# Idle matmuls in the opening of a two-stage kernel, and the token keys of its second group moved ahead of the third's

## The chip, the core and the metric

The kernel runs on one core of a Trainium2 chip. A core has a matrix engine (TensorE, PE in the rows, with its weight loads as PEld), a vector engine (DVE), a scalar engine (ACT), a third elementwise engine (POOL), and an engine that here only issues transfers (SP). Each works through its own list of instructions in order and waits on semaphores for the others. The metric is the device time of one execution in microseconds; the kernel before takes 529.84 us, the median of three runs (529.17 to 530.13).

## The reference

The first stage is a linear attention over 4 batches, 8 heads, 768 steps and head size 48; its output is the input of a gated network with 3072 tokens, model width 384 and inner width 1536.

```python
for t in range(S):
    cur = einsum('bhd,bhe->bhde', u[None] * k[:, :, t], v[:, :, t])
    y[:, :, t] = einsum('bhd,bhde->bhe', r[:, :, t], state + cur)
    state = w[None, :, :, None] * state + einsum('bhd,bhe->bhde', k[:, :, t], v[:, :, t])
x = y.transpose(0, 2, 1, 3).reshape(B * S, H * D)
gate = 1 / (1 + exp(-(x @ w_gate)))
out = (gate * (x @ w_val)) @ w_out
```

All of it is in float32.

## The kernel before

The 768 steps are cut into 12 chunks of 64. One chunk of one half of the heads is a group, so there are 24 groups; they are numbered 0, 1, 2, ... in the order in which they are worked on. For each group n the following steps exist, and the letters are those of the table `START` in the code:

- `L` and `X` load its channels (queries and keys with the channel on the partitions, tile `chan`) and its tokens (keys and values with the token on the partitions, tile `toks`).
- `A`, `R`, `k`, `T` scale them by powers of the decay: bonus keys on ACT (line 287), queries on POOL or DVE (line 293), keys on DVE (line 304), token keys on POOL or DVE (line 308). `T` writes its result over the keys in `toks`.
- `Z` computes the scores on PE (line 375), `K` copies those under the mask to the tile `score` on DVE (line 383).
- `I` applies them to the values, from group 2 on with the part that comes from the state, and `O` forms the outer product of token keys and values for the next state; both are on PE at line 337. `O` needs the token keys of `T`.
- `h` and `l` round the output to the high part of the network's input on ACT (line 474) and take the rest as the low part on DVE (line 478); `s` and `d` renew and decay the state; `F` moves some rows of the input to other partitions by six transfers (line 482).

The network works in 12 blocks f of the inner width. `W` loads the block's weights, which come as whole 64-bit words, `c` (ACT, line 240) and `j` (DVE, line 247) turn them to float32, `w` (ACT, line 255) rounds them to a high part and `o` (POOL or DVE, line 258) forms the low part. `U` is the up projection, 18 matmuls at line 516: nine for the gate and nine for the value, each a product of a high or low part of the weights with a high or low part of the input. `g`, `m`, `H`, `q` are the gating on ACT, DVE, ACT and POOL or DVE, and `D` is the down projection (line 554). For the first two blocks the first tile of 512 tokens is worked on in two halves of 256, since its second half is computed later.

The order of the work is written out by hand. The first part of it, up to the end of the first 512 tokens, is the table `START`, a list of steps that are issued one after the other; each engine gets its instructions in this order and keeps it. Then a loop goes through the other five tiles of tokens with a fixed pattern: up projection, the attention of a later group in the first, fourth, seventh and tenth block, gating, and the down projection of the block before. In the listing `tc` is the step that makes the constants, the identity matrix `ident` among them, `tt` four transposes for the table of token powers on PE (line 197), and `tn` the copy of that table, which every `T` needs.

Of the loads, SP issues all. The scheduling layer gives the transfers eight semaphores in turn, and a transfer is issued when the one eight places ahead of it has landed.

Of the kernel before, what the change touches and what calls it, by code (L numbers as in the profile page):

```python
# [10 lines left out]
F32 = mybir.dt.float32  # L11
# [32 lines left out]
L.0 W.0 L.1 X.0 W.1 L.2 X.1 X.2 tc A.0 tk ti.1 R.0 ti.0 k.0 tp tr Z.0 tt K.0 I.0 c0.0 A.1 c0.1 tn  # L44
h.0 c.1 T.2 T.1 k.1 Rv.1 j0.1 l.0 Tv.0 j0.0 Z.1 O.0 W.2 F.0 W.3 L.3 L.4 W.4 X.3 j.1 K.1 I.1 O.1 A.2
w0.0 sa.0 w.1 h.1 w0.1 o0.1 o.1 R.3 Rv.2 k.2 o0v.0 l.1 s.1 Z.2 K.2 U.0 I.2 O.2 g.0 c.2 d.2 A.3 m.0
U.1 H.0 g.1 h.2 j.2 k.3 s.2 l.2 q.0 T.3 m.1 F.2 L.5 W.8 X.4 L.6 W.5 W.6 L.7 X.5 F.1 X.6 L.8 W.7 Z.3
K.3 I.3 O.3 w.2 A.4 k.4 H.1 c.3 h.3 l.3 R.4 D.0 Z.4 U.2 d.3 s.3 g.2 c.4 j.3 w.3 j.4 qv.1 m.2 o.2
U.4 H.2 g.4 w.4 A.5 K.4 q.2 U.3 D.2 g.3 Rv.5 m.3 k.5 ov.3 m.4 T.4 I.4 O.4 Z.5 H.3 A.6 d.4 h.4 H.4
c.6 c.5 k.6 s.4 K.5 l.4 Tv.5 j.6 R.6 q.3 D.1 D.3 U.5 I.5 g.5 h.5 j.5 qv.4 l.5 m.5 o.4 Z.6 D.4 R.7  # L50
O.5 U.6 A.7 d.5 H.5 K.6 k.7 s.5 q.5 T.6 w.5 ov.5 U.7 c.8 c.7 g.6 j.7 m.6 L.9 X.8 ub Y.8 W.9 W.10
X.7 I.6 Z.7 O.6 D.5 w.6 g.7 ov.6 d.6 w.7 H.6 s.6 j.8 qv.6 h.6 l.6 m.7 w.8 ov.7 H.7 qv.7 D.6 U.8 K.7
R.8 c.9 ov.8 g.8 m.8 Tv.7 H.8 U.9 qv.8 g.9 k.8 j.9 w.9 o.9 m.9 D.7 U.10 g.10 H.9 c.10 j.10 m.10 q.9
D.8 I.7 H.10 d.7 Z.8 O.7 h.7 w.10 D.9 s.7 U.11 ov.10 l.7 W.11 F.5 X.9 F.6 F.3 F.7 F.4 Y.9 qv.10
g.11 c.11 j.11 D.10 U.12 m.11 w.11 R.9 ov.11 U.13 g.12 H.11 qv.11 m.12 H.12 qv.12 g.13 t.8 D.11 b.8
i.8 D.12 K.8 k.9 m.13 H.13 q.13 b.9 T.9 t.9 i.9 T.8
# [4 lines left out]
def rwkv_then_moe(ctx: ExitStack, tc: tile.TileContext, wd, ub, ch, tk, rt, wt, rk0, vn0, wd0, out):  # L61
# [38 lines left out]
    def load_channels(n):  # L100
        c, g = GROUPS[n]
        chan[n] = ach.tile([P, 2, 512], F32, name="chan")
        nc.sync.dma_start(out=chan[n], in_=ch[c, g])  # L103

    def load_tokens(n):
        c, g = GROUPS[n]
        toks[n] = atk.tile([P, 2, TKW], F32, name="toks")
        nc.sync.dma_start(out=toks[n], in_=tk[c, g])  # L108
# [15 lines left out]
    def constants():  # L124
        make_identity(nc, ident)
        nc.gpsimd.memset(causal, 0.0)
# [7 lines left out]
        for t in score:  # L134
            nc.gpsimd.memset(t, 0.0)
        nc.gpsimd.memset(state, 0.0)
        nc.scalar.activation(table, ident[:, 0:1], AF.Sigmoid)
        nc.vector.memset(tops[0].rearrange("q n two -> q (n two)").bitcast(F32), 0.0)
        nc.gpsimd.memset(tops[1].rearrange("q n two -> q (n two)").bitcast(F32), 0.0)


# [109 lines left out]
    def round_weights(f, c):  # L251
# [3 lines left out]
        nc.scalar.copy(out=whi[f][:, c], in_=w32[f][:, c])  # L255
# [34 lines left out]

    def queries(n, eng=nc.gpsimd):
# [210 lines left out]
    class Moe:  # L502
# [3 lines left out]

        def up(self, f):
            w = whi[f], wlo[f]
            self.pair[f] = []
            for g in range(2):  # L510
                o = one_bank()
                self.pair[f].append(o)
                k = 0
                for kt in range(3):
                    for a, b in PASS:
                        nc.tensor.matmul(  # L516
                            o[:, self.cols], w[a][:, g * DM + kt * P : g * DM + (kt + 1) * P],
                            self.x[:, kt, b, self.cols], start=(k == 0), stop=(k == 8),
                        )
                        k += 1  # L520
# [73 lines left out]
    halves = [(0, g) for g in range(HALF)] + [(1, g) for g in range(HALF)] + [(2, g) for g in range(HALF, NF)]  # L594
    items = [(0, h, f) for h, f in halves]
    n0 = len(items)
# [24 lines left out]
    def idle_matmuls(k):  # L621
        t = pacc.tile([P, 512], F32, name="acc2")
        for _ in range(k):
            nc.tensor.matmul(t[:, 0:P], ident, ident, start=True, stop=True)

    steps = {
        "b": own_tokens, "i": diagonal, "ub": lambda: load_bonus(),
        "N": idle_matmuls,
        "L": load_channels, "X": load_tokens, "Y": load_own, "W": load_weights, "A": bonus_keys, "R": queries, "t": turn_queries,
        "k": keys, "T": token_keys, "Z": scores, "K": keep, "I": apply, "O": outer,  # L630
        "d": decay_state, "s": add_state, "h": x_high, "l": x_low, "F": fills, "D": finish,
# [260 lines left out]
```

## Time and profile before

| what | value |
|---|---|
| time, median of 3 runs | 529.84 us (529.17 to 530.13) |
| the profiled execution's own time | 529.63 us |
| its span, from the first to the last instruction | 527.8 us |
| PE busy | 506.9 us, 96% of the span |
| PEld, DVE, ACT, POOL busy | 422.0, 202.7, 186.2, 188.4 us |
| DMA queue of the loads, share of 16 engines | 25.3% |

The span is 1.8 us shorter than the time of the same execution; the rest lies ahead of the first and behind the last instruction. Times in rows count from the start of the span. In a timeline a row merges instructions of one kind that follow each other: start, time from the first's start to the last's end, engine, line, operation, operands, shape and count, and in brackets the idle time ahead of them with what ended it. A float32 matmul of a score or an outer product stands in the program once and in the trace as two records, so a group of 16 matmuls shows as x32.

### The profile page before, as it was taken

What the parts mean: (1) busy time and instruction counts of PE and PEld (TensorE: products, weight loads), DVE (VectorE), ACT (ScalarE), POOL (GpSimd) and SP (SyncE); (2) the same over time, 40 slices, a digit from 0 to 9 for tenths busy, and PEclk for the clock granted to TensorE, in tenths of its full rate; (3) what the DMA queues carried; (4) which work ended last, traced back from release to release, by engine and by line L of the source; (5) the groups of instructions that cost most, each with busy time, mean ns of one, the idle gap of its engine ahead of it and who ended that gap; (6) DMA issues with size and microseconds to landing.
All of it is one profiled execution on the core that took longest, in us unless ns stands there. A gap on an engine that the chain in (4) does not pass through costs nothing.

```text
span 527.8 us, 11947 instructions
## 1 busy us (share of the span) xinstructions
PE 506.9 (96%) x5204; PEld 422.0 (80%) x5204; DVE 202.7 (38%) x345; ACT 186.2 (35%) x395; POOL 188.4 (36%) x158
## 2 busy tenths in 40 slices
PE   3689999999999999999999999999999999999995
PEld 3679888888888788888888888888888888888884
DVE  8877856555242243242341432331442211111112
ACT  5587764544223134233233332331432221211211
POOL 4463512314555252453442452552353111111220
PEclk9999999999999999999999999999999999999998
DMA  8939744122212030420230420311400000100001
GB/s 328 363 131 418 268 170 187 24 85 84 79 74 76 22 107 2 145 87 17 81 102 8 146 88 0 98 37 71 147 17 2 11 10 11 61 0 1 0 2 65
DMA packets 15579, 47.84 MB, mean 91 GB/s; under 512 B 2368, under 2 KB 4928, under 8 KB 14112
## 3 DMA queue, kind: packets, MB, share of 16 engines
q1 hardware_dynamic: 15376, 46.74, 25.3%
q8 instruction: 43, 0.70, 0.6%
q10 hardware_dynamic: 144, 0.26, 0.1%
q14 instruction: 16, 0.13, 0.1%
HBM read 39.92 MB, written 4.72 MB: 85 GB/s over the span
## 4 chain that ended last, share of the span: by engine, by line
PE 94%; DMA 2%; SPq 1%; DVE 1%; issue 1%; POOL 0%; ACT 0%; DVEq 0%; POOLq 0%
PE ring L516 56%; PE acc L554 29%; PE ring L337 7%; PE sc L375 2%; DMA toks<-in_tk 2%; DVE xt L478 0%; DVE score L383 0%; POOL toks L308 0%; SPq L233 0%; SPq L103 0%; SPq L108 0%; ACT xt L474 0%; DVE sg L567 0%; SPq L95 0%; ACT sg L525 0%
## 5 line engine op out<-in xcount | busy, mean ns | idle before, releaser
L516 PE MATMUL ring<-xt,wx 128*128 128x512 f32 (+1 forms) x1332 | 308.1, 385 | 0.7 <-ACT sg L525 0.5
L516 PEld LDWEIGHTS ring<-xt,wx 128*128 128x128 f32 x1332 | 246.7, 189 | 50.5 <-ACT sg L525 0.7
L538 POOL TENSOR_TENSOR h<-sg,h 128x512 fp32r<-128x512 f32 (+1 forms) x65 | 87.2, 1342 | 253.8 <-ACT h L534 253.8
L554 PE MATMUL acc<-h,wx 128*128 128x512 f32 (+1 forms) x666 | 161.3, 387 | 0.0
L554 PEld LDWEIGHTS acc<-h,wx 128*128 128x128 f32 x666 | 121.2, 188 | 24.9 <-DVE h L538 0.2
L529 DVE TENSOR_TENSOR sg<-ring,sg 128x512 f32<-128x512 f32 (+1 forms) x74 | 50.0, 675 | 237.5 <-PE ring L516 236.0
L525 ACT ACTIVATE sg<-ring 128x512 f32<-128x512 f32 (+1 forms) x74 | 43.3, 585 | 155.3 <-PE ring L516 155.3
L534 ACT CAST h<-sg 128x512 fp32r<-128x512 f32 (+1 forms) x74 | 45.0, 608 | 144.2 <-DVE sg L529 138.0
L293 POOL TENSOR_TENSOR dec<-chan,tabk 128x512 f32<-128x512 f32 x21 | 27.8, 1325 | 13.8 <-PE ring L337 13.7
L478 DVE TENSOR_TENSOR xt<-ring,xt 112x256 fp32r<-112x256 f32 (+1 forms) x52 | 19.9, 418 | 32.8 <-ACT xt L474 32.7
L308 POOL TENSOR_TENSOR toks<-toks,tabn 128x384 f32<-128x384 f32 x19 | 24.8, 1308 | 11.5 <-DMA toks<-in_tk 11.5
L314 POOL TENSOR_TENSOR dec<-dec,toks 128x384 f32<-128x384 f32 x16 | 16.3, 1018 | 26.4 <-DMA dec<-in_rt 26.3
L375 PE MATMUL sc<-dec,chan 48*64 48x64 f32 x768 | 17.4, 231 | 7.7 <-DVE chan L304 7.6
L304 DVE TENSOR_TENSOR chan<-chan,tabk 128x512 f32<-128x512 f32 x24 | 24.7, 1027 | 0.1
L383 DVE COPY_PREDICATED score<-masks,sc 128x512 f32<-128x512 int32 x32 | 23.9, 746 | 1.8 <-PE sc L375 1.1
L428 ACT ACTIVATE state<-state,pw 112x96 f32<-112x96 f32 x80 | 23.4, 363 | 1.9 <-PE ring L337 1.8
L337 PE MATMUL ring<-score,toks 64*48 64x64 f32 (+1 forms) x768 | 16.7, 226 | 5.0 <-DVE score L383 4.1
L375 PEld LDWEIGHTS sc<-dec,chan 48*64 48x64 f32 x768 | 15.0, 145 | 8.1 <-POOL dec L293 7.6
L247 DVE SCALAR_TENSOR_TENSOR wf<-wr,top 128x1152 int32<-128x1152 int32 (+1 forms) x13 | 17.3, 1342 | 10.4 <-ACT top L240 6.9
L447 DVE TENSOR_TENSOR state<-state,ring 48x192 f32<-48x192 f32 (+1 forms) x52 | 17.9, 350 | 8.4 <-PE ring L337 4.6
L474 ACT CAST xt<-ring 112x256 fp32r<-112x256 f32 (+1 forms) x52 | 16.7, 364 | 9.0 <-PE ring L337 8.8
L337 PEld LDWEIGHTS ring<-score,toks 64*48 64x48 f32 (+1 forms) x768 | 14.3, 134 | 6.4 <-DVE score L383 4.8
(59 smaller groups left out, 247.1 us busy)
## 6 DMA issues: line engine op xcount, KB each, us to landing
wr<-in_wt SPq DMA_DIRECT2D x11, 1152.0 KB, 8.8
chan<-in_ch SPq DMA_DIRECT2D x24, 512.0 KB, 4.3
toks<-in_tk SPq DMA_DIRECT2D x24, 400.0 KB, 5.0
out_y<-wf SPq DMA_DIRECT2D x16, 256.0 KB, 2.4
dec<-in_rt SPq DMA_DIRECT2D x16, 192.0 KB, 2.7
xt<-xt SPq DMA_DIRECT2D x30, 64.0 KB, 2.3
wr<-in_wt SPq DMA_DIRECT2D x2, 576.0 KB, 5.2
xt<-xt SPq DMA_DIRECT2D x12, 32.0 KB, 3.9
```

The source lines that it names most:

```text
L293: eng.tensor_tensor(v4(t[:, 0]), v4(chan[n][:, 0]), bc2(table_of(n)[:, :, ::-1]), ALU.mult)
L304: nc.vector.tensor_tensor(v4(k), v4(k), bc2(table_of(n)), ALU.mult)
L308: eng.tensor_tensor(v4(k), v4(k), bc2(tabn[:, 4 * g : 4 * g + 4]), ALU.mult)
L337: nc.tensor.matmul(yb[n][bank][64 * half : 64 * half + m, cs], lhsT, rhs, start=first, stop=stop, skip_group_check=True,)
L375: nc.tensor.matmul(sc[64 * gm : 64 * gm + 64, be, o : o + C], kk[row, cs : cs + C], rr[row, cs : cs + C], start=True, stop=True,)
L383: nc.vector.copy_predicated(t.rearrange("q (b m i) -> q b m i", b=2, m=4), masks[:, m].bitcast(I32).unsqueeze(1).unsqueeze(1).broadcast_to ...
L516: nc.tensor.matmul(o[:, self.cols], w[a][:, g * DM + kt * P : g * DM + (kt + 1) * P], self.x[:, kt, b, self.cols], start=(k == 0), stop=(k ...
L525: nc.scalar.activation(sg[:, c], self.pair[f][0][:, c], AF.Sigmoid, scale=UP)
L529: nc.vector.tensor_tensor(sg[:, c], self.pair.pop(f)[1][:, c], sg[:, c], ALU.mult)
L534: nc.scalar.copy(out=h[:, 0, c], in_=sg[:, c])
L538: eng.tensor_tensor(h[:, 1, c], self.sg.pop(f)[:, c], h[:, 0, c], ALU.subtract)
L554: nc.tensor.matmul(self.acc[d][:, self.cols], w[a][:, 2 * DM + d * P : 2 * DM + (d + 1) * P], h[:, b, self.cols], start=(f == 0 and k == 0 ...
```

## The change

Four things in the code are different.

- The table `START` gets 30 matmuls of the identity with itself (step `N`, function `idle_matmuls`, which was there and was not used): 13 ahead of the first scores, then 3, 2, 1, 6, 2, 1 and 2 in front of the transposes, the scores of group 1, the outer product of group 0, the applied scores of group 1, its outer product, the scores of group 2 and the first up projection. They write to the bank of the third accumulator, which nothing reads before the first down projection starts it anew.
- In the table the token keys of group 1 (`T.1`) come before those of group 2 (`T.2`); before it was the other way round.
- The step that makes the constants is split into small ones, named one by one in the table in the same order on each engine; the up projection is split into its gate part `u` and value part `v`; and blocks are named by block and half (`0a`, `0b`, `2`) and not by a running number. Some functions take the engine as an argument, with the old one as default.
- Far later, ACT issues one copy of the state ahead of one rounding of the gated product; they changed places.

The diff, with the table cut to its first lines:

```diff
 START = """
-L.0 W.0 L.1 X.0 W.1 L.2 X.1 X.2 tc A.0 tk ti.1 R.0 ti.0 k.0 tp tr Z.0 tt K.0 I.0 c0.0 A.1 c0.1 tn
-h.0 c.1 T.2 T.1 k.1 Rv.1 j0.1 l.0 Tv.0 j0.0 Z.1 O.0 W.2 F.0 W.3 L.3 L.4 W.4 X.3 j.1 K.1 I.1 O.1 A.2
+ta L.0 tov.0 tc tb W.0 ts.0 L.1 ts.1 X.0 tz W.1 tk L.2 X.1 to.1 ti.1 X.2 ti.0 A.0 R.0 N.13 W.2 k.0
+c0.0 tp Z.0 tr N.3 tt A.1 K.0 I.0 c0.1 k.1 tn Rv.1 h.0 N.2 j0.1 Z.1 l.0 N.1 Tv.0 O.0 j0.0 c.1 N.6
+A.2 j.1 w0.0 T.1 sa.0 F.0 T.2 W.3 K.1 w.1 Rv.2 I.1 N.2 k.2 O.1 N.1 o0v.0 L.3 L.4 Z.2 W.4 N.2 X.3 h.1
...
-        def up(self, f):
-            w = whi[f], wlo[f]
-            self.pair[f] = []
-            for g in range(2):
-                o = one_bank()
...
+        def up_one(self, f, g):
+            w, o, k = (whi[f], wlo[f]), one_bank(), 0
+            self.pair.setdefault(f, []).append(o)
...
+        def up(self, f):
+            self.up_one(f, 0)
+            self.up_one(f, 1)
...
     def idle_matmuls(k):
-        t = pacc.tile([P, 512], F32, name="acc2")
+        t = accs[0][2] if 0 in accs else pacc.tile([P, 512], F32, name="acc2")
         for _ in range(k):
             nc.tensor.matmul(t[:, 0:P], ident, ident, start=True, stop=True)
...
+    moe_steps = {
+        "U": Moe.up, "u": lambda m, f: m.up_one(f, 0), "v": lambda m, f: m.up_one(f, 1), "g": Moe.sigmoid, "m": Moe.product, "H": Moe.h_high, "q": Moe.h_low,
+        "qv": lambda m, f: m.h_low(f, nc.vector),
     }
     for step in START.split():
         name, _, arg = step.partition(".")
-        steps[name](*([int(arg)] if arg else []))
+        if name == "D":
+            finish(block(arg))
+        elif name in moe_steps:
+            moe_steps[name](moe_of(block(arg)), block(arg)[2])
+        else:
+            steps[name](*([int(arg)] if arg else []))
```

On PE at the start of the program, before (line 375 is the first scores, 197 the transposes, 337 the applied scores of group 0):

```order
L887 UNCONDITIONAL_BRANCH
L375 MATMUL sc<-dec,chan 64x64 x16
L375 MATMUL sc<-chan,dec 64x64 x16
L197 MATMUL acc_201<-spare,sg 128x128 x4
L337 MATMUL ring<-score_97,toks 64x64 x2
```

and now (line 636 is the idle matmuls; 389, 204 and 351 are the old 375, 197 and 337):

```order
L917 UNCONDITIONAL_BRANCH
L636 MATMUL acc_161<-spare 128x128 x13
L389 MATMUL sc<-dec,chan 64x64 x16
L389 MATMUL sc<-chan,dec 64x64 x16
L636 MATMUL acc_218<-spare 128x128 x3
L204 MATMUL acc_222<-spare,sg 128x128 x4
L351 MATMUL ring<-score_97,toks 64x64 x2
```

Nothing that stood there changed places; the idle matmuls stand between.

On PE from the applied scores of group 1 (`score_98`) to the first up projection, before:

```order
L337 MATMUL ring<-score_98,toks 64x64 x2
L337 MATMUL ring<-score_98,toks 48x64 x2
...
L337 MATMUL ring<-toks 64x48 x2
L337 MATMUL ring<-toks 48x48 x2
...
L375 MATMUL sc<-dec,chan 64x64 x16
L375 MATMUL sc<-chan,dec 64x64 x16
L516 MATMUL ring<-xt,wx 128x256 x18
```

and now (526 is the old 516, the up projection):

```order
L636 MATMUL acc_320<-spare 128x128 x6
L351 MATMUL ring<-score_98,toks 64x64 x2
L351 MATMUL ring<-score_98,toks 48x64 x2
...
L636 MATMUL acc_371<-spare 128x128 x2
L351 MATMUL ring<-toks 64x48 x2
L351 MATMUL ring<-toks 48x48 x2
...
L636 MATMUL acc_391<-spare 128x128
L389 MATMUL sc<-dec,chan 64x64 x16
L389 MATMUL sc<-chan,dec 64x64 x16
L636 MATMUL acc_433<-spare 128x128 x2
L526 MATMUL ring<-xt,wx 128x256 x18
```

Again the old matmuls keep their order, with eleven idle ones between them.

On POOL, with the tiles' numbers, before (`toks_123` are the tokens of group 1, `toks_125` those of group 2, line 258 the low part of the first blocks' weights):

```order
L293 TENSOR_TENSOR dec_145<-chan_110,tabk_102 128x512
L308 TENSOR_TENSOR toks_125<-toks_125,tabn_103 128x384
L308 TENSOR_TENSOR toks_123<-toks_123,tabn_103 128x384
L258 TENSOR_TENSOR wx_358<-wf_242,wx_358 128x576
L258 TENSOR_TENSOR wx_362<-wf_315,wx_362 128x1152
```

and now (`toks_148` are the tokens of group 1, `toks_152` those of group 2):

```order
L307 TENSOR_TENSOR dec_155<-chan_114,tabk_102 128x512
L322 TENSOR_TENSOR toks_148<-toks_148,tabn_103 128x384
L322 TENSOR_TENSOR toks_152<-toks_152,tabn_103 128x384
L265 TENSOR_TENSOR wx_334<-wf_262,wx_334 128x576
L265 TENSOR_TENSOR wx_350<-wf_332,wx_350 128x1152
```

The two token keys changed places; all else on POOL, and everything on DVE and SP, stands as before.

## Rows read from the trace of the kernel before

**Rows 1.** Page, part 1: busy us, share of the span, instructions

```profile
PE 506.9 (96%) x5204; PEld 422.0 (80%) x5204; DVE 202.7 (38%) x345; ACT 186.2 (35%) x395; POOL 188.4 (36%) x158
```

**Rows 2.** The chain that ended last: start us, us, what

```profile
20.41 1.15 PE ring L337 x24
...
33.76 0.76 DVE score L383
...
38.83 8.72 PE ring L516 x54
```

**Rows 3.** Stretches: length, busy of each engine (records), granted clock, DMA share, GB/s

```profile
60.00:80.00 20.00, 19.82 (x284) 16.18 (x275) 14.05 (x21) 15.06 (x29) 5.14 (x4) 1.00 0.51 186
...
7.62:15.33 7.71, 6.98 (x196) 6.14 (x196) 7.14 (x15) 5.19 (x13) 0.00 (x0) 1.00 1.03 422
24.13:26.86 2.73, 2.73 (x12) 2.73 (x13) 2.11 (x4) 0.82 (x2) 2.73 (x2) 1.00 1.03 396
...
30.35:33.76 3.41, 2.94 (x95) 2.60 (x98) 2.31 (x7) 3.19 (x9) 3.06 (x3) 1.00 0.04 10
```

**Rows 4.** Timeline of PE from the first scores to the first down projection

```profile
7.62 1.13 PE L375 MATMUL sc<-dec,chan 48*64 48x64 f32 x32 [7.62 <-DVE chan L304]
...
17.59 1.12 PE L337 MATMUL ring<-score,toks 64*64 64x64 f32 x32 [2.25 <-DVE score L383]
...
24.14 3.36 PE L516 MATMUL ring<-xt,wx 128*128 128x256 f32 x16 [0.18 <-DVE xt L478]
27.43 0.68 PE L337 MATMUL ring<-dec,state 48*64 48x64 f32 x32
...
35.35 0.68 PE L337 MATMUL ring<-score,toks 64*64 64x64 f32 x32 [1.19 <-DVE score L383]
```

**Rows 5.** Lines 516 and 197: duration ns min/median/max, first and last start

```profile
L516 PE MATMUL ring<-xt,wx x10: 415/415/416, 24.5 to 26.4; 128*128 128x256 f32 x10
...
L516 PE MATMUL ring<-xt,wx x9: 279/282/389, 29.5 to 30.5; 128*128 128x256 f32 x9
...
L197 PE MATMUL acc<-spare,sg x4: 417/418/473, 9.5 to 10.2; 128*128 128x128 f32 x4
```

**Rows 6.** Timeline of DVE, ACT and POOL around the same work

```profile
1.02 0.29 POOL masks.py:199 TENSOR_SCALAR_AFFINE_SELECT spare<-spare 128x128 f32<-128x128 f32 x1
...
14.11 2.02 DVE L247 SCALAR_TENSOR_TENSOR wf<-wr,top 128x576 int32<-128x576 int32 x2
16.05 1.49 DVE L383 COPY_PREDICATED score<-masks,sc 128x512 f32<-128x512 int32 x2
...
17.49 2.86 POOL L308 TENSOR_TENSOR toks<-toks,tabn 128x384 f32<-128x384 f32 x2 [10.52 <-DMA toks<-in_tk]
18.01 1.49 DVE L304 TENSOR_TENSOR chan<-chan,tabk 128x512 f32<-128x512 f32 x1
...
21.57 1.51 ACT L474 CAST xt<-ring 48x256 fp32r<-48x256 f32 x4 [3.88 <-PE ring L337]
22.35 1.73 DVE L478 TENSOR_TENSOR xt<-ring,xt 48x256 fp32r<-48x256 f32 x4 [1.39 <-ACT xt L474]
23.86 4.04 POOL L258 TENSOR_TENSOR wx<-wf,wx 128x576 fp32r<-128x576 f32 x2 [3.51 <-ACT wx L255]
24.76 1.54 DVE L383 COPY_PREDICATED score<-masks,sc 128x512 f32<-128x512 int32 x2
...
27.86 1.27 POOL L293 TENSOR_TENSOR dec<-chan,tabk 128x512 f32<-128x512 f32 x1
27.94 2.41 DVE L247 SCALAR_TENSOR_TENSOR wf<-wr,top 128x1152 int32<-128x1152 int32 x1
```

**Rows 7.** Transfers issued at 4.69, 17.53 and 22.52: KB, us to landing

```profile
toks<-in_tk SPq DMA_DIRECT2D x1, 400.0 KB, 10.4
...
xt<-xt SPq DMA_DIRECT2D x1, 32.0 KB, 4.6
...
toks<-in_tk SPq DMA_DIRECT2D x1, 400.0 KB, 8.9
```

More of the change, by code (lines that the diff above doesn't have):

```diff
@@ L122, in rwkv_then_moe, with identity, causal_masks @@
     table = const.tile([P, 1], F32, name="table")
-    def constants():
+    def identity():
         make_identity(nc, ident)
+    def causal_masks():
         nc.gpsimd.memset(causal, 0.0)
@@ L133, in constants, with clear_scores, clear_state, first_table @@
             nc.gpsimd.tensor_copy(masks[lo : lo + 64, 1], ident[lo : lo + 64, lo : lo + 64])
-        for t in score:
-            nc.gpsimd.memset(t, 0.0)
-        nc.gpsimd.memset(state, 0.0)
+    def clear_scores(i, eng=nc.gpsimd):
+        eng.memset(score[i], 0.0)
+    def clear_state(eng=nc.gpsimd):
+        eng.memset(state, 0.0)
+    def first_table():
         nc.scalar.activation(table, ident[:, 0:1], AF.Sigmoid)
-        nc.vector.memset(tops[0].rearrange("q n two -> q (n two)").bitcast(F32), 0.0)
-        nc.gpsimd.memset(tops[1].rearrange("q n two -> q (n two)").bitcast(F32), 0.0)
+    def clear_top(i, eng=nc.gpsimd):
+        eng.memset(tops[i].rearrange("q n two -> q (n two)").bitcast(F32), 0.0)
     pw = const.tile([P, N2, 97], F32, name="pw")
@@ L249, in join_words, with round_weights @@
         )
-    def round_weights(f, c):
+    def round_weights(f, c, copy=nc.scalar.copy):
         if f not in wparts:
@@ L254, in round_weights @@
             whi[f], wlo[f] = wparts[f][:, 0:W3], wparts[f][:, W3 : 2 * W3]
[L255 removed]
+        copy(out=whi[f][:, c], in_=w32[f][:, c])
     def rest_of_weights(f, c, eng=nc.gpsimd):
@@ L470, in x_of, with x_high @@
         ]
-    def x_high(n):
+    def x_high(n, copy=nc.scalar.copy):
         for x, y in x_of(n, 0):
-            nc.scalar.copy(out=x, in_=y)
+            copy(out=x, in_=y)
     def x_low(n):
@@ L505, in __init__ @@
             self.pair, self.sg, self.h = {}, {}, {}
-        def up(self, f):
-            w = whi[f], wlo[f]
-            self.pair[f] = []
-            for g in range(2):
-                o = one_bank()
[L512 to L520, printed above, removed]
+        def up_one(self, f, g):
+            w, o, k = (whi[f], wlo[f]), one_bank(), 0
+            self.pair.setdefault(f, []).append(o)
+            for kt in range(3):
+                for a, b in PASS:
+                    nc.tensor.matmul(
+                        o[:, self.cols], w[a][:, g * DM + kt * P : g * DM + (kt + 1) * P],
+                        self.x[:, kt, b, self.cols], start=(k == 0), stop=(k == 8),
+                    )
+                    k += 1
+        def up(self, f):
+            self.up_one(f, 0)
+            self.up_one(f, 1)
         def sigmoid(self, f):
@@ L591, in store_last @@
             )
-    halves = [(0, g) for g in range(HALF)] + [(1, g) for g in range(HALF)] + [(2, g) for g in range(HALF, NF)]
-    items = [(0, h, f) for h, f in halves]
-    n0 = len(items)
+    items = [(0, 2, NF - 1)]
     for ti in range(1, len(TILES)):
@@ L641, in rwkv_then_moe, with block @@
         "Rv": lambda n: queries(n, nc.vector), "Tv": lambda n: token_keys(n, nc.vector),
[L642 to L647 removed]
+    }
+    def block(arg):
+        return (0, "ab".index(arg[-1]), int(arg[:-1])) if arg[-1] in "ab" else (0, 2, int(arg))
+    moe_steps = {
+        "U": Moe.up, "u": lambda m, f: m.up_one(f, 0), "v": lambda m, f: m.up_one(f, 1), "g": Moe.sigmoid, "m": Moe.product, "H": Moe.h_high, "q": Moe.h_low,
+        "qv": lambda m, f: m.h_low(f, nc.vector),
     }
@@ L672, in rwkv_then_moe @@
     load(n + 2)
-    for i in range(n0, len(items)):
+    for i in range(1, len(items)):
         ti, h, f = items[i]
```

91 lines of the change are left out of this document (51 added, 40 removed).

## The prediction

> **What bounds the kernel now.** I read the page first: PE is busy for 506.9 of 527.8 us [rows 1], so only its remaining 21 us, and matmuls that run slower than they could, can be won. Then the stretches: from 60 us on PE is busy for 19.8 of 20 us and more [rows 3], and in the chain of waits PE work follows PE work from 38.83 us on [rows 2]. So what the opening gives is read at that place: if the block at 38.83 us starts earlier by some time and nothing behind it runs dry, the kernel ends earlier by as much. Ahead of it the chain runs through the token keys on POOL, a pair that starts at 17.49 us when the tokens of group 2 have landed [rows 6] and in which those of group 1 stand second, and the outer product of group 1 at 20.41 us [rows 2].
>
> Third, the timeline of PE with the durations. A group of 32 records of the small matmuls takes 1.13 us at 7.62 and 0.68 us at 27.43 [rows 4]. Up to 26.4 us the matmuls of 256 columns start every (26.4 - 24.5)/9 = 0.21 us, and from 29.5 us every (30.5 - 29.5)/8 = 0.12 us [rows 5]. [...] The column of the granted clock reads 1.00 all the while [rows 3], so here only the durations tell the level. From 24.13 to 26.86 us PE was busy without a break with matmuls of 128 x 128 weights and 256 columns [rows 3, 4], and after that the rate is the high one.
>
> **The change part by part.** *Renamed steps, split constants, u and v.* Every engine but PE, POOL and ACT keeps its list, and ACT's one swap lies where PE never idles: nothing.
>
> *Thirteen idle matmuls at the start.* The identity is made at 1.02 + 0.29 = 1.3 us [rows 6], and the first scores wait for DVE until 7.62 us [rows 4], so PE has 6.3 us free. The trace of before has no idle matmul; the nearest is the four transposes of 128 columns, spaced by (10.2 - 9.5)/3 = 0.23 us at the low level [rows 5]. A float32 matmul leaves two records where a transpose leaves one. So one idle matmul costs between 0.23 and 0.46 us at the low level and half of that at the high one, and 13 cost at most 6.0 us: done at 7.3 us, in free time. I take the upper value.
>
> *Seventeen in the pauses.* At the high level 0.23 us each. Twelve (3, 2, 1, 6) stand ahead of the applied scores of group 1, 2.8 us against a pause of 2.25 us there [rows 4], 7.71 - 6.98 = 0.73 us of pauses ahead of it [rows 3], and six groups that each shrink by 1.13 - 0.68 = 0.45 us: covered. Two (0.46 us) stand between applied scores and outer product of group 1, where nothing hides them once the pause there is gone. One stands ahead of the scores of group 2, two ahead of the up projection, where other waits end later (below).
>
> *Token keys swapped, with the high level kept.* DVE ends the scores' copy for group 1 at 16.05 + 1.49 = 17.54 us, as before: its list ahead is full, behind weights that have to land. The applied scores take 17.59 to 18.27, the two idle ones end at 18.73. The tokens of group 1 land at 4.69 + 10.4 = 15.1 us [rows 7]. Its token keys then meet the joining of weights on DVE, 14.11 to 16.13 us, and end by 17.5 us even if they start only behind that (half of the pair's 2.86 us is 1.4 us [rows 6], so from 16.1 to 17.5). So the outer product runs from 18.73 to 19.4 us, where before it started at 20.41. ACT's cast, which waits for it, starts at 19.4 in place of 21.57 us, 2.2 us earlier, and DVE's low part, now 22.35 to 24.08 us, ends at 21.9.
>
> The first up projection needs this, the scores of group 2 ahead of it on PE, and the six moved rows. The keys of group 2 end at 18.01 + 1.49 = 19.5 us as before; the scores take two groups, 19.6 to 20.8, two idle ones to 21.3. The last moved rows land at 17.53 + 4.6 = 22.1 us [rows 7], which the change can't move, as they queue behind weights; only the seventh matmul needs them, and starting with the third at 21.9 it comes at 22.3. Sixteen matmuls of 0.12 us end at 24.0 us, where the sixteen of before end at 27.5 [rows 4]: 1.5 us of this is the level, the rest the earlier start. The copy of the next scores on DVE ended at 24.76 + 1.54 = 26.30 us, 2.2 us behind the low part [rows 6], so now at 24.1. The applied scores of group 2 start at 24.1 and not at 27.43: **3.3 us earlier**.
>
> From there the path forks. POOL's two weight parts (23.86 + 4.04 = 27.90 us) start behind ACT, 2.2 us earlier, so they end at 25.7, and the queries behind them at 27.0 us. The next joining of weights on DVE took 2.41 us beside those queries; the second one of the row at 14.11 has the same 1152 columns, twice those of the first, and took two thirds of 2.02, or 1.35 us, with POOL idle [rows 6]. So the queries blocked it, and again it ends 1.2 us behind them, at 28.2 us, 2.2 us earlier than 27.94 + 2.41 = 30.35. From there to the copy of the scores of group 3, at 33.76 us [rows 2], DVE was busy for 2.31 of 3.41 us and else waited for PE and ACT [rows 3], which now are 3.3 us ahead. So that copy can start at 28.2 + 2.3 = 30.5 us. That is **3.2 us earlier**, and the applied scores of group 3 start at 32.1 in place of 35.35 us [rows 4]. Their outer product, half a microsecond behind, needs tokens that land at 22.52 + 8.9 = 31.4 us whatever PE does [rows 7]; with 1.4 us at most on POOL they are ready by 32.8, just in time. That caps any gain near 3.4 us. The second set of moved rows, and the loads queued behind it on SP, wait for a low part on DVE that stands between the joining and that copy, so they come 2.2 to 3.2 us earlier.
>
> So the block at 38.83 us starts between 2.2 (if the loads decide) and 3.2 us (if PE does) earlier. I take the middle, **2.7 us**: 529.63 - 2.7 = 526.9 us against the profiled execution's own time, and as the median of the runs is 0.2 us above that, **527.1 us**.
>
> *Who goes first on DVE and POOL.* The joining at 27.94 us, begun 0.08 us behind POOL's queries, took 2.41 and not 1.35 us, and so did the keys at 18.01 us, 1.49 us beside the pair of token keys [rows 6]: of two such instructions the earlier one goes first. At 15.1 us DVE's joining (from 14.8) is ahead of the token keys, if nothing delays it. If POOL is first, the joining ends 1.0 us later, 1.2 of the 2.2 us at the cast are left, and the end comes near **528.0 us**. [...]
>
> **The rivals.** *The level is never lifted early, and the idle matmuls stand in the way (slower).* For it: from 7.62 to 15.33 us PE was busy for 6.98 of 7.71 us and the next group still took 1.12 us [rows 3, 4]: the level had not risen. Against it: what ran ahead of the rise were matmuls with 128 x 128 weights, and so are the idle ones. Price: at 0.46 us each the twelve ahead of the applied scores of group 1 take 5.5 us against 2.25 + 0.73 us of pauses, so these start 2.5 us late, at 20.1; with two more (0.9) the outer product starts at 22.1, 1.7 us late in spite of the swap, and three more (1.4) bring the up projection to some 2.5 us behind 24.14. At 0.23 us the twelve fit the pauses and nothing is lost. I take 1.4 us, a little over the middle: **531.0 us**. It decides from the point where the applied scores of group 1 start after 18.6 us, since from there their outer product, 1.8 us behind, is no earlier than it was.
>
> *Lifted at the start, lost again before the first up projection.* For it: pauses of up to 1.8 us remain, ahead of the applied scores of group 1. Against it: after the pause of 1.19 us at 35.35 the matmuls still ran at the high rate [rows 4]. [...] Price: applied scores 17.6 to 18.7, two idle ones at 0.46, outer product to 20.7 where it ended at 21.5, so 0.8 us are won at the cast; then two groups of scores (2.0) and three idle ones (1.4) fill PE until 24.1, and the 16 matmuls take 3.36 us as before. Between 0.5 us won and 0.5 us lost is left: **529.8 us**, the median of before.
>
> **How the numbers follow.** The forecast has a chance of 0.70, POOL winning the port 0.06, the level lost again 0.13, the idle matmuls in the way 0.11. What the measurement can tell from no change is about 0.2%, 1.06 us, so faster means below 528.8. Faster: 0.68 of the first, 0.05 of the second, 0.01 of the third, 0.74. The same: 0.02 + 0.01 + 0.11 + 0.02 = 0.16. Slower: 0.10. The forecast's own range is 526.1 (the cap of 3.4 us, and the 0.4 us by which runs differ) to 528.2; to hold 8 in 10 it reaches to the rival that loses the level: 526.1 to 529.9 us.
>
> **What would show it.** Right: the first scores take 0.7 us per group, the outer product of group 1 starts near 18.7, the first up projection spaces its matmuls by 0.12 us and ends near 24.0, and the steady stretch, now from 38.83 us, begins near 36 us. Wrong: small groups of 1.1 us behind the first idle matmuls, the cast still near 21.6 us, or new pauses of PE behind 38 us, where loads that didn't move would be late.

## The result, and the profile after

The changed kernel takes 537.34 us (median of 6 runs, 535.97 to 539.45), the kernel before beside it 529.59 us: the ratio is 1.0146, with a 95% interval of 1.0129 to 1.0162. It is slower by 1.5%, where 527.1 us was forecast and 526.1 to 529.9 given as the range. The profiled execution took 535.97 us, with a span of 534.2 us, the fastest of the six; against the 527.8 us of before 6.4 us are to be found in it.

The page's first part answers to [rows 1]: thirty float32 matmuls are 60 records more, and PE is busy for 8 us more. The fetches of instructions have a queue of their own in the third part of the page.

```profile
PE 514.9 (96%) x5264; PEld 427.7 (80%) x5264; DVE 203.2 (38%) x345; ACT 186.2 (35%) x395; POOL 188.9 (35%) x158
...
q8 instruction: 43, 0.70, 0.5%
```

The timeline of PE after, for the places of [rows 4]: start, length, line, what, and in brackets the idle time ahead of it and what ended it.

```profile
1.37 5.92 PE L636 MATMUL acc<-spare 128*128 128x128 f32 x26 [1.37 <-POOL spare masks.py:199]
7.63 0.69 PE L389 MATMUL sc<-dec,chan 48*64 48x64 f32 x32 [0.34 <-issue]
...
19.05 0.68 PE L351 MATMUL ring<-score,toks 64*64 64x64 f32 x32 [2.73 <-DVE score L397]
...
23.61 2.18 PE L526 MATMUL ring<-xt,wx 128*128 128x256 f32 x16 [0.25 <-DVE xt L492]
25.72 0.68 PE L351 MATMUL ring<-dec,state 48*64 48x64 f32 x32
...
33.06 0.43 PE L351 MATMUL ring<-dec,state 48*48 48x64 f32 x12 [0.74 <-issue]
...
50.62 0.98 PE L568 MATMUL acc<-h,wx 128*128 128x256 f32 x6
54.58 2.40 PE L568 MATMUL acc<-h,wx 128*128 128x256 f32 x12 [2.97 <-issue]
...
81.03 0.73 PE L568 MATMUL acc<-h,wx 128*128 128x512 f32 x2 [0.46 <-ACT h L548]
...
107.49 1.38 PE L526 MATMUL ring<-xt,wx 128*128 128x512 f32 x5 [1.11 <-DVE xt L492]
```

The rate of PE, the level of the prediction, is lifted as forecast: the first scores take 0.69 us per group, not 1.13. The first up projection ends at 25.8 us, 1.7 us earlier than before, though not at 24.0. The chain of waits then shows what became of it; it answers to the last row of [rows 2], and its first row to the last transfer of [rows 7].

```profile
24.15 9.18 DMA toks<-in_tk
...
38.05 8.72 PE ring L526 x54
...
51.61 2.97 issue
```

The tokens of group 3, issued at 24.15 us and not at 22.52, land at 33.3 us, 2.0 us later than before, and of the 1.7 us won at the up projection the block that started at 38.83 us keeps 0.78: it starts at 38.05. At 51.61 us PE stops in the middle of a down projection, between its sixth and seventh record of 18, for 2.97 us, labelled "issue": it waited for no semaphore that the profile shows. The stretches around it (length, then busy time of PE, PEld, DVE, ACT and POOL with their records, granted clock, DMA share, GB/s):

```profile
44.00:51.60 7.60, 7.45 (x196) 6.95 (x195) 5.78 (x10) 6.15 (x18) 4.71 (x5) 1.00 1.01 424
51.61:54.58 2.97, 0.00 (x1) 0.00 (x0) 2.30 (x6) 0.00 (x0) 2.46 (x1) 1.00 1.06 413
54.58:58.42 3.84, 3.84 (x16) 3.52 (x16) 1.68 (x2) 3.29 (x3) 0.00 (x0) 0.56 0.75 312
```

The DMA engines are full before and during the stop, and behind it the granted clock is 0.56 in the mean, 0.50 from 55.0 to 58.4 us (the low level: most matmuls of 256 columns take 0.415 us there, and 0.283 us ahead of the stop), after PE had done nothing for 2.97 us.

Laid side by side, the starts of the 74 up projections of line 526 against those of line 516 give the account. The shift is -0.28 and -1.71 us at the first two places, then -0.78 us from the block of 38.83 us up to the stop; +3.12 at the next one, in which the stop and part of the low level are; +3.89 behind that; +4.63 from 83 us; +5.99 from 107 us; +6.63 from 145 us, and so to the last of them. So the steps are 3.90 + 0.77 (the stop and the low level), 0.74, 1.36 and 0.64 us.

The 0.74 and 1.36 us are two waits of PE, 0.46 us at 81.03 and 1.11 us at 107.49. Both come from ACT: at 107.49 us PE waits for DVE's low part, which stands behind an instruction of DVE that waited 2.01 us for ACT's rounding of the weights (the last two rows below). ACT's timeline before, a first and a second place, and after, the same two:

```profile
74.10 0.61 ACT L534 CAST h<-sg 128x512 fp32r<-128x512 f32 x1
75.73 0.71 ACT L453 COPY state<-spare 48x192 f32<-48x192 f32 x2 [1.02 <-DVE spare L447]
...
98.05 1.18 ACT L255 CAST wx<-wf 128x1152 fp32r<-128x1152 f32 x1
99.11 0.72 ACT L453 COPY state<-spare 48x192 f32<-48x192 f32 x2
```

```profile
79.63 0.72 ACT L467 COPY state<-spare 48x192 f32<-48x192 f32 x2 [1.54 <-DVE spare L461]
80.36 0.62 ACT L548 CAST h<-sg 128x512 fp32r<-128x512 f32 x1
...
103.73 0.71 ACT L467 COPY state<-spare 48x192 f32<-48x192 f32 x2 [0.93 <-DVE spare L461]
104.46 1.16 ACT L262 CAST wx<-wf 128x1152 fp32r<-128x1152 f32 x1
...
105.65 1.36 DVE L265 TENSOR_TENSOR wx<-wf,wx 128x1152 fp32r<-128x1152 f32 x1 [2.01 <-ACT wx L262]
106.92 0.75 DVE L492 TENSOR_TENSOR xt<-ring,xt 112x256 fp32r<-112x256 f32 x2
```

The cast that stood ahead of the copies of the state stands behind them now, and the copies wait for DVE. There are two such swaps, and not the one of which the section on the change and the prediction spoke: the second one moves a rounding of weights.

### The profile page after: what moved, and what is told of

Read it like the earlier page. It is cut to its first block, busy times and chain, and to the rows that moved or that the text cites. A ratio compares the mean times of both kernels' runs of the same rounds, so it can differ in the third digit from the quotient of the medians.

```text
span 534.2 us, 12066 instructions
## 1 busy us (share of the span) xinstructions
PE 514.9 (96%) x5264; PEld 427.7 (80%) x5264; DVE 203.2 (38%) x345; ACT 186.2 (35%) x395; POOL 188.9 (35%) x158
## 4 chain that ended last, share of the span: by engine, by line
PE 89%; DMA 4%; DVE 2%; POOL 1%; issue 1%; ACT 1%; SPq 1%; POOLq 0%; DVEq 0%; ACTq 0%
PE ring L526 53%; PE acc L568 27%; PE ring L351 6%; PE sc L389 2%; DMA wr<-in_wt 2%; DMA toks<-in_tk 2%; DMA dec<-in_rt 1%; POOL toks L322 0%; SPq L240 0%; DVE score L397 0%; ACT top L247 0%; POOL h L552 0%; DVE wf L254 0%; ACT state L442 0%; DVE state L461 0%
## 5 line engine op out<-in xcount | busy, mean ns | idle before, releaser
L322 POOL TENSOR_TENSOR toks<-toks,tabn 128x384 f32<-128x384 f32 x19 | 25.3, 1336 | 13.2 <-DMA toks<-in_tk 13.2
L247 ACT ACTIVATE top<-wr 128x1152 f16<-128x1152 bf16 (+1 forms) x13 | 18.1, 1416 | 2.6 <-DMA wr<-in_wt 2.6
L265 POOL TENSOR_TENSOR wx<-wf,wx 128x1152 fp32r<-128x1152 f32 (+1 forms) x5 | 12.0, 2409 | 19.3 <-ACT wx L262 19.3
L351 PEld LDWEIGHTS ring<-dec,state 48*64 48x64 f32 (+1 forms) x448 | 12.1, 131 | 7.8 <-issue 7.6
```

Of the source, the lines that this page charges most:

```text
L322: eng.tensor_tensor(v4(k), v4(k), bc2(tabn[:, 4 * g : 4 * g + 4]), ALU.mult)
L351: nc.tensor.matmul(yb[n][bank][64 * half : 64 * half + m, cs], lhsT, rhs, start=first, stop=stop, skip_group_check=True,)
```

## Experiments

Theory F: PE's instructions are fetched in pieces (the trace of the change has 43 packets of 16,384 B in the instruction queue), a piece is late where the loads fill the DMA engines and PE has run through a burst of small matmuls, and the thirty idle matmuls shift the places where pieces begin. Rival A: ACT's order is the whole loss. Rival C: the work of the idle matmuls does it. Rival L: loads that land late. Each ratio is to the kernel before, run beside the experiment (529.91 us with 1 to 4, 529.98 with 5 to 8, 530.36 with 9 and 10), and each kernel has one profiled execution. All kernels are the changed one with the edits shown, which stand in the table of the start. "ACT back" is this edit:

```diff
-g.5 v.5 I.6 Y.8 R.8 Z.7 W.9 d.6 O.6 W.10 X.7 w.7 s.6 W.11 X.9 H.4 j.8 D.3 h.6 qv.4 l.6 w.8 m.5 D.4
+g.5 v.5 I.6 Y.8 R.8 Z.7 W.9 d.6 O.6 W.10 X.7 w.7 H.4 s.6 W.11 X.9 j.8 D.3 h.6 qv.4 l.6 w.8 m.5 D.4
...
-g.8 H.7 v.8 q.7 c.10 D.6 j.10 m.8 I.7 H.8 Z.8 O.7 d.7 R.9 h.7 s.7 D.7 b.8 w.10 u.9 ov.10 g.9 l.7
+g.8 H.7 v.8 q.7 c.10 D.6 j.10 m.8 I.7 H.8 Z.8 O.7 d.7 R.9 h.7 w.10 s.7 D.7 b.8 u.9 ov.10 g.9 l.7
```

**1. No idle matmuls** (all eight N steps gone, the first of them shown):

```diff
-ta L.0 tov.0 tc tb W.0 ts.0 L.1 ts.1 X.0 tz W.1 tk L.2 X.1 to.1 ti.1 X.2 ti.0 A.0 R.0 N.13 W.2 k.0
+ta L.0 tov.0 tc tb W.0 ts.0 L.1 ts.1 X.0 tz W.1 tk L.2 X.1 to.1 ti.1 X.2 ti.0 A.0 R.0 W.2 k.0
...
```

> The changed kernel without the thirty idle matmuls (its two ScalarE swaps and the token-key swap stay). Theory F (the loss is a stall in TensorE's supply of instructions: the thirty matmuls shift which instruction is the first that is not there yet, and 2.97 us of 'issue' at 51.61 with the low clock after it cost about 4.6): no idle of TensorE over 1 us labelled 'issue' between 45 and 60 us; what is left is the two ScalarE swaps (0.74 + 1.36 us), so about 529.6 + 2.1 = 531.7, down to 530 if the token-key swap gives something. Rival A (the ScalarE order alone, growing with the run): 536 to 538 as with them. Rival L (the loads, which landed 0.6 to 1.9 us later in the changed kernel's profile): 533 or more, with the first weights landing at 14.6.

Measured 531.13 us, 1.0024 (1.0011 to 1.0036) of before. The list of PE's waits from 38 us to the end (line, releaser: us in total, times, longest) has the two of ACT's order and no long "issue":

```profile
PE ring L526 <- DVE xt L492: 1.1, 1, 1.1
PE ring L351 <- issue: 0.5, 3, 0.2
PE acc L568 <- ACT h L548: 0.5, 1, 0.5
```

The stop comes with the idle matmuls. A is refuted as the whole: 6.2 of the 7.8 us went with them. L is not decided here, as weights 1 landed at 13.1 us again and not at 14.6; experiment 5 decides it.

**2. ACT back**, the thirty kept (the edit above).

> The changed kernel with both ScalarE swaps undone (h's rounding ahead of the state copies at 79.6 us, the weights' rounding ahead of them at 103.7). Theory F: the stall at 51.6 us stays, the waits of 0.46 us at 81.0 and of 1.11 us at 107.5 go: 537.3 - 2.1 = 535.2 (534.7 to 535.8). Rival A: back to 529 to 531. Rival that neither wait is ScalarE's order: 537.3 as before.

Measured 535.55 us, 1.0096 (1.0076 to 1.0116). The same list: the two waits are gone, the stop stays.

```profile
PE acc L568 <- issue: 2.9, 1, 2.9
PE acc L568 <- POOL h L552: 0.8, 1, 0.8
```

537.34 - 535.55 = 1.8 us is what the two swaps cost with the matmuls, 531.13 - 529.25 = 1.9 us without (the next run), against 0.74 + 1.36 = 2.1 by the shifts.

**3. Token keys alone** (no N step, ACT back).

> The kernel before with the token-key swap alone (no idle matmul, ScalarE order of before). Theory F: no stall, clock low until 26.9 as in the kernel before; the swap lets the outer product of group 1 start up to 1.3 us earlier (POOL's token keys 1.34 us each), but the first up projection is held by the weights' rounding, so 528.5 to 529.8. Rival that the swap itself does the harm: over 531.

Measured 529.25 us, 0.9984 (0.9971 to 0.9998): the swap of the token keys gives 0.16%, no harm.

**4. Idle matmuls alone** (thirty, ACT back, token keys of before):

```diff
-A.2 j.1 w0.0 T.1 sa.0 F.0 T.2 W.3 K.1 w.1 Rv.2 I.1 N.2 k.2 O.1 N.1 o0v.0 L.3 L.4 Z.2 W.4 N.2 X.3 h.1
+A.2 j.1 w0.0 T.2 T.1 sa.0 F.0 W.3 K.1 w.1 Rv.2 I.1 N.2 k.2 O.1 N.1 o0v.0 L.3 L.4 Z.2 W.4 N.2 X.3 h.1
```

> The kernel before with the thirty idle matmuls alone (token keys and ScalarE in the order of before). Theory F: the clock is high from 7 us, a TensorE gap of 1 to 3 us labelled 'issue' stands somewhere between 30 and 60 us, and the time is 529.6 + 3.9 + 0.8 less up to 1 for the faster opening: 533 to 535. Rival A: 526 to 529. Rival that idle matmuls help nothing and cost nothing: 529.6.

Measured 536.08 us, 1.0110 (1.0076 to 1.0145), a little over the expected range. The stop is 2.92 us, inside the same down projection. By the shift of the up projections the stop and the low level behind it cost 5.5 us in the profiled execution (537.63 us), 1.9 us were lost in the opening, and 0.7 us at a wait at 146 us. The opening, in PE's stretches (length, busy, records, granted clock, DMA share, GB/s):

```profile
16.00:20.00 4.00, 1.20 (x35) 0.79 1.00 339
20.00:24.00 4.00, 4.00 (x82) 0.50 0.90 307
24.00:28.00 4.00, 4.00 (x54) 0.50 1.02 409
```

Here PE lost the high level in the pause of 2.80 us ahead of the applied scores of group 1, and did the first up projection at a granted clock of 0.50: the rival "lost again" came true in this execution, and in the one of experiment 2 (0.50 from 20 to 24 us), while the profiled one of the change kept the level. The spread of the change's six runs goes with the clock: from 0.996 and 535.97 us, the profiled run, every slower run has the same or a lower granted clock, down to 0.984 and 539.45 us. At which place those runs lost it is not on record.

**5. The number of instructions, meant to be without the work.** No N step and ACT back, and in place of the thirteen thirty matmuls of two columns:

```diff
+            nc.tensor.matmul(t[:, 0:2], ident, ident[:, 0:2], start=True, stop=True)
...
-... ti.1 X.2 ti.0 A.0 R.0 N.13 W.2 k.0
+... ti.1 X.2 ti.0 A.0 R.0 n.30 W.2 k.0
```

> The kernel with the token keys alone, and thirty matmuls of two columns ahead of the first scores in place of the thirty of 128 (the same number of instructions on TensorE at the same places of the rest, almost no work and no work in the pauses). Theory F: the gap of about 2.9 us labelled 'issue' is back inside the same down projection (after its sixth record), and the time is that kernel's 529.3 + 3.9 to 4.8 = 533.2 to 534.1. Rival C (the idle matmuls' work, through the clock or the bank they write, does the harm): no gap, 529.3.

Measured 542.22 us, 1.0232 (1.0207 to 1.0256). The stop is there, in the same place of the program, but the time was mis-sized: two columns cost nearly what 128 do (0.216 us per record, against 5.92 / 26 = 0.228 us in the change).

```profile
1.38 12.96 PE L641 MATMUL acc<-spare 128*128 128x2 f32 x60 [1.38 <-POOL spare masks.py:199]
...
58.49 0.98 PE L568 MATMUL acc<-h,wx 128*128 128x256 f32 x6
62.42 2.93 PE L568 MATMUL acc<-h,wx 128*128 128x256 f32 x12 [2.95 <-issue]
```

12.96 us went into the opening (the shift against before is 7.1 us at the block of 38.83 us and 13.0 us behind the stop). The stop came at the same record 8 us later than in the change (59.5 against 51.6 us), so it hangs on the place in the program, and not on the time, on the high level (a group takes 1.08 to 1.14 us here up to 26 us) or on matmuls in the pauses. Weights 1 landed at 13.1 us, as early as in experiment 1, and the stop is there all the same: L is refuted as its cause. The idle work is still there, so C is left to the next experiment.

**6. A whole piece of instructions.** ACT back, the thirty kept and 34 of two columns ahead of them (n.34 N.13).

> The thirty idle matmuls of the change, ScalarE order of before, and 34 more of two columns ahead of them: 64 matmuls, 256 instructions, which is what one instruction packet of 16384 B holds if an instruction has 64 B (43 packets against 10,528 matmul and weight-load records in the changed kernel's page). Theory F: where the fetch stands at each later instruction is as in the kernel before, so no gap over 0.5 us labelled 'issue' at 45 to 60 us; without it 535.55 - 4.2 = 531.3, 527 to 529 where the clock also stays high through the opening. Rival C: 535.5 or more. Rival that every added instruction costs: 536 or more.

Measured 542.13 us, 1.0226 (1.0201 to 1.0252), mis-sized in the same way: the 34 take 14.67 us. The down projection runs through:

```profile
63.68 2.42 PE L568 MATMUL acc<-h,wx 128*128 128x256 f32 x18
```

More instructions and more idle work on the same bank, and no stop here: the shift against before is 12.28 us ahead of this place and 12.28 us behind. So C is refuted. Beyond the 12.28 us that the idle matmuls fill in the opening it is not their count that costs but where it puts the start of a piece: "every added instruction costs" gave the right range, but not by its mechanism.

**7. Thirteen idle matmuls** (the other seven N steps gone, ACT back).

> Only the thirteen idle matmuls ahead of the first scores (52 instructions in place of 120), token keys as in the change, ScalarE order of before. Theory F: the first missing instruction comes 17 matmuls (68 instructions) later, at 12 records of the down projection and 22 of the up projection behind it, some 2.3 + 8 us later than the gap was, so that the fetch is there: no gap over 1 us at 50 to 62 us; 527.5 to 529.5, as the clock can be lost in the pauses without the seventeen. Rival C (idle work): 533 or more.

Measured 528.79 us, 0.9971 (0.9957 to 0.9985). PE stops once, elsewhere:

```profile
58.91 0.73 PE L568 MATMUL acc<-h,wx 128*128 128x512 f32 x2
60.43 1.78 PE L568 MATMUL acc<-h,wx 128*128 128x512 f32 x7 [0.79 <-issue]
```

Counted from the start, 978 records of PE lie ahead of the stop in the change and in experiments 2, 4, 5 and 8, and 1104 here: 126 apart, 252 instructions with their weight loads. The high level was lost here too, from 12.3 to 25.9 us (granted clock 0.50 from 16 to 24 us): without the seventeen the opening is at the low level as before from there on.

**8. Loads later.** ACT back, thirty kept:

```diff
-... L.6 D.0a W.5 W.6 l.3
+... L.6 D.0a l.3
...
-... L.8 d.4 D.1a W.7
+... L.8 W.6 W.5 d.4 D.1a W.7
```

> The changed kernel with the ScalarE order of before, and with the loads of weights 5 and 6 issued behind the load of channels 8 (which waits for TensorE until 50.8 us) in place of at 38.4 and 39.0. Theory F, with the fetch waiting in line behind loads (the packet went at 52.12, when the load of weights 6 had landed at 52.24): the DMA engines are free at about 50 us, the fetch is there earlier and the gap shrinks from 2.9 us to under 1: 535.55 - 3 to 4 = 531.5 to 532.5, less if the weights 5 land after 57.2 us, where they are first read. Rival (a fetch of fixed length that starts too late whatever the loads do): gap and time unchanged, 535.5.

Measured 539.34 us, 1.0183 (1.0159 to 1.0208). The stop shrank as F said; the time, forecast at 531.5 to 532.5 us, did not, as the weights are now late for ACT, and PE waits behind it:

```profile
52.06 1.58 PE L567 MATMUL acc<-h,wx 128*128 128x256 f32 x12 [0.64 <-issue]
...
63.22 1.11 PE L350 MATMUL ring<-dec,state 48*64 48x64 f32 x30 [5.21 <-ACT sg L538]
```

ACT's waits from 45 to 66 us name what it lacked:

```profile
ACT top L246 <- DMA wr<-in_wt: 6.5, 2, 3.6
```

With the same instructions the stop is 0.64 us in place of the 2.89 us of experiment 2: some 2.2 us of it were the wait behind the loads. The 0.64 us are left where the DMA engines were nearly idle (share 0.06 to 0.07 from 48 to 50 us, 0.00 from 50 to 51 us).

**9. Ten idle matmuls, six of them wide.** ACT back, and N and M steps as follows:

```diff
+                t.rearrange("q (a x) -> q a x", a=4), ident,
+                ident.unsqueeze(1).broadcast_to([P, 4, P]), start=True, stop=True,
...
-... A.0 R.0 N.13 W.2 k.0
+... A.0 R.0 M.3 N.1 W.2 k.0
-c0.0 tp Z.0 tr N.3 tt A.1 K.0 I.0 c0.1 k.1 tn Rv.1 h.0 N.2 j0.1 Z.1 l.0 N.1 Tv.0 O.0 j0.0 c.1 N.6
+c0.0 tp Z.0 tr N.1 tt N.1 A.1 K.0 I.0 c0.1 k.1 tn Rv.1 h.0 N.1 j0.1 Z.1 l.0 Tv.0 O.0 j0.0 c.1 M.3
...
```

> Ten idle matmuls in place of thirty, six of them 512 columns wide (three ahead of the first scores, three in the pause ahead of the second applied scores) and four of 128 (40 instructions in place of 120), token keys as in the change, ScalarE order of before. Theory F: with 20 records more than the kernel before the instructions missed at 51.6 us (60 records) and at 60.43 us (26 records, 0.79 us) come late enough: no gap over 0.3 us labelled 'issue' after 45 us; the clock high from about 7 us, the first up projection some 1.5 us before the kernel before's, 526.5 to 528.5, the fastest here. Rival that an added instruction costs in proportion: between the 528.8 of thirteen and that of none. Rival C (idle work does the harm, more columns more harm): 533 or more.

Measured 527.17 us, 0.9954 (0.9937 to 0.9970): faster than both kernels. There is no "issue" over 0.3 us behind 38 us, and the level holds:

```profile
1.37 5.49 PE L641 MATMUL acc<-spare 128*128 128x512 f32 x6 [1.37 <-POOL spare masks.py:199]
...
17.63 0.70 PE L351 MATMUL ring<-score,toks 64*64 64x64 f32 x32 [0.33 <-DVE score L397]
...
21.64 2.45 PE L526 MATMUL ring<-xt,wx 128*128 128x256 f32 x18 [0.87 <-DMA xt<-xt]
24.02 0.68 PE L351 MATMUL ring<-dec,state 48*64 48x64 f32 x32
```

**10. Twenty-one idle matmuls** (N.13, N.6 and the N.2 ahead of O.1 stay, ACT back).

> Twenty-one idle matmuls of 128 columns (13, 6 and 2; 84 instructions), token keys as in the change, ScalarE order of before. Theory F, with the place fixed by the number of the instruction: the record numbers at which TensorE ran dry were 978 (30 idle matmuls, 2.9 us) and 1104 (13, 0.79 us); with 42 records the record 978 lies 18 records later in the program than with 60, a gap of 0 to 1 us there, and one of 0.5 to 2.5 us at record 1104; 529.5 to 533, between the thirteen and the thirty. Rival (a gap grows with the count of idle matmuls at one place of the program): a gap of 2 us inside the down projection after its sixth record, and none at 1104.

Measured 532.31 us, 1.0057 (1.0034 to 1.0081). The stops are at records 978, 1104 and 1359 (255 behind, twice the distance and 3 more):

```profile
55.28 3.01 PE L526 MATMUL ring<-xt,wx 128*128 128x512 f32 x12 [0.16 <-issue]
...
60.75 0.46 PE L389 MATMUL sc<-chan,dec 48*64 48x64 f32 x14 [0.21 <-issue]
...
77.21 0.96 PE L568 MATMUL acc<-h,wx 128*128 128x512 f32 x3 [0.77 <-issue]
```

The places are those that F names, the sizes at 1104 less than expected, and the stop at 77 us was not foreseen. A theory that lets one stop grow at one place of the program is refuted. The high level was lost here as well, from 10.5 to 20.8 us.

**The packets beside the stops.** The traces settle how a stop and a fetch hang together. In the twelve executions PE has fourteen stops labelled "issue" at a record number of this series: 222, 600, 726, 978, 1104 and 1359, which are 126 or a multiple of it apart; only 1359 lies 3 further. (In the change the 0.74 us at 33.06 us is one, at record 600; it cost nothing, as the block behind it waited for the tokens of group 3 anyway.) Each of the fourteen ends 1.27 to 1.50 us after a packet of 16,384 B of the instruction queue has landed. The other "issue" rows of PE behind 20 us are of 0.29 us or less and stand at places where kernels without a stop have them too.

The size of the stop follows as well. In the change the piece ahead of the stop, 126 records, begins at 48.77 us. The packet starts 3.35 us after that, takes 1.07 us, and PE goes on 1.39 us behind it: 5.81 us. PE is through the 126 records, nearly all of small matmuls, in 2.84 us, and the difference is the stop of 2.97 us. In experiment 8, with the DMA engines nearly idle, the packet starts after 0.95 us, and 0.95 + 1.10 + 1.42 - 2.83 = 0.64 us is the stop there. In the kernel before the same record numbers, 852 to 977, take 7.95 us, as an up projection stands among them, and there is no stop. What sets off a fetch no record shows; the start of the piece ahead is taken here as the place to count from.

## Why the prediction was wrong

**The step that failed** is "nothing behind it runs dry". The prediction took a gain in the opening to arrive at the end whole. PE did run dry, of instructions, which neither an engine nor a load shows as a wait: 4.67 us (3.90 + 0.77) of stop and low level, in place of nothing. The thirty matmuls were priced by their time alone, and that price was right for the thirteen (5.92 us against the 6.0 us forecast). Their 120 instructions were not priced at all. Of the signs of being wrong, "new pauses of PE behind 38 us" came true, though the loads that were to make them did not.

Against the forecast of 526.9 us the profiled execution is 9.1 us longer: 4.67 us by the stop, 2.10 us by ACT's order, 1.9 us by the opening, which gave 0.78 and not 2.7 us, and 0.64 us by the wait at 144 us make 9.3 us, of which 0.3 us come back behind the last matmul.

The runs show how large a piece is: 43 packets of 16,384 B stand in the trace beside 2 x 5264 = 10,528 records of matmuls and weight loads, 245 to a packet; the 256 instructions more of experiment 6, against the kernel before, come with a 44th packet; and the stops lie 126 records, 252 instructions, apart, which makes an instruction 16,384 / 252 = 65 B by estimate, near the 64 B with which experiment 6 was sized. Most pieces came without a stop: in the change PE stood at two of these places, 0.74 us at record 600 and 2.97 us at record 978.

**"One swap of ACT: nothing."** There were two swaps, and they cost 1.8 us of the median. "Where PE never idles" was read as room; it means the reverse, that whatever is late there is late at the end.

**"DVE ends the scores' copy for group 1 at 17.54 us, as before."** It ended at 18.99, and the applied scores started at 19.05 (forecast 17.59). That is behind the 18.6 us that the prediction gave as the sign of its slow rival, though the level was high; so the outer product of group 1 started at 20.30 us (forecast 18.73, before 20.41) and ACT's cast at 21.05 (forecast 19.4, before 21.57), and the swap of the token keys gained next to nothing. The weights that stand ahead of it on ACT and DVE landed later. The transfers of both profiled executions from 11.0 to 13.2 us (queue: packets, MB, share), and the landing time of weights 1, first of before, then of after:

```profile
q1 hardware_dynamic: 191, 0.90, 98.1%
...
wr<-in_wt SPq DMA_DIRECT2D x1, 1152.0 KB, 9.2
```

```profile
q1 hardware_dynamic: 155, 0.87, 95.4%
q8 instruction: 1, 0.02, 3.0%
...
wr<-in_wt SPq DMA_DIRECT2D x1, 1152.0 KB, 10.7
```

In the change a piece of instructions is fetched from 11.9 us on (before: from 14.8), while weights 1 are on their way, and they land 10.7 us after their issue in place of 9.2. In all twelve profiled executions the two go together: the change and experiments 2, 4 and 8 have a packet ending at 13.0 us and weights 1 at 14.2 to 14.6 us; in the others the first packet ends at 15.0 us or later and weights 1 land by 13.4. Before, that packet ended at 15.8 us, behind weights 1. In experiments 7 and 10 it went from 14.0 to 15.1 us, and the tokens of group 1, which were in flight then, took 11.9 us to land in place of 10.4. No experiment moved that packet alone, so this stands on its coming together twelve times out of twelve. The longer pause (2.73 us; 2.81 in experiment 2, 2.80 in experiment 4) is also the one around which the level was lost there: in experiment 4 at 18.3 us, within it, and in experiment 2 at 19.7 us, 0.6 us behind it (0.79 and 0.96 as the mean granted clock from 16 to 20 us).

**The cap** from the tokens of group 3, forecast at 31.4 us "whatever PE does", moved to 33.3 us in the change, so the loads decided, at 0.78 us. In experiment 9 they landed at 31.7, and the loads decided there too: PE's path to the block runs through these tokens.

**What held.** The high level from the thirteen matmuls on (0.69 us per group; "never lifted" is refuted). The path through token keys, outer product and low part: where no piece of instructions came in its way, in experiment 9, the applied scores of group 1 started at 17.63 us (forecast 17.59), the first up projection ended at 24.1 (24.0), the block of 38.83 us came 2.48 us earlier (2.7, of 2.2 if the loads decide to 3.2), and the time was 527.17 us, 3.2 us under the 530.36 of before beside it. So the mechanism of the opening was sized well, and it was worth 0.5%. That the number meets the 527.1 us forecast is in part luck, as that was for thirty matmuls and another order of ACT. The seventeen in the pauses were covered as said, but the pause behind them grew; their price of half the low level's was an estimate, and the six ahead of the applied scores of group 1 took 1.60 us, 0.27 each and not 0.23.

**"If POOL is first"** did not show as a cost: DVE's joining started at 16.21 us, POOL's token keys at 16.93, and the joining took 1.36 us. No run shows a port between the two engines; what the two traces show is that the later of two such instructions took longer: before, the joining at 27.94 us, 2.41 and not 1.35 us behind POOL's queries, and in the change these queries, from 27.35 us, 2.40 and not 1.27 us behind a joining that started at 26.64. The 0.64 us at 144 us is a wait for h's low part behind a load of 192 KB that took 4.1 us to land in place of 2.7, with a piece of instructions fetched beside it (a packet at 136.5 us); a wait of 0.3 to 0.8 us is at that place in experiments 2, 4 and 8 too, and in none of 1, 3, 6, 7, 9 and 10. That the packet causes it was not tried.

## What to carry over

Instructions that only fill idle time were not free here: thirty idle matmuls, 120 instructions, moved the later places where a piece of PE's program begins, and one of these, at record 978, fell behind a burst of small matmuls while the loads filled the DMA engines (share 1.01 to 1.06), for 2.97 us. Look for idle time labelled "issue" in the middle of a loop, count the records up to it, and try a few more or fewer before the idea itself is given up: here, with ACT's order of before, the same idea was 1.0% slower with thirty matmuls (experiment 2) and 0.5% faster with ten. Use few wide instructions where work is only meant to keep an engine busy (six records of 512 columns filled 5.49 us in experiment 9, 26 of 128 columns 5.92 us in the change), and never call a reordering free on a stretch where the bounding engine has no slack.

## What the runs showed of the hardware

A float32 matmul with a weight load of 128 x 128 costs 12.96 / 60 = 0.216 us per record with 2 columns, 5.92 / 26 = 0.228 us with 128 and 5.49 / 6 = 0.915 us with 512, all at the low level ahead of the first rise (at the high level, from 14.45 us in experiment 9, 2.84 / 6 = 0.473 us with 512): from 2 to 128 columns the time grew by 0.012 us only. The granted clock, which read 1.00 throughout the opening of before at the low level, does read 0.50 to 0.79 where a level once reached is lost again (experiment 4). And a pause of 2.7 to 2.8 us was followed by the loss of the high level in two executions and not in a third, while in experiments 7 and 10 it was lost at 12.3 and 10.5 us, in experiment 7 with PE busy since 7.6 us in pieces with pauses of at most 0.9 us between them.
